# V^T of three quads packed into four transposes instead of six, at the end of their own quad

## The chip, the cores and the metric

The kernel runs on one core of one Trainium2 chip. The metric is the device time of one execution in microseconds (us). The kernel before takes 3127.38 us, the median of three runs (3127.18 to 3128.78). A core has five engines that matter here: TensorE (PE, with its weight loads as PEld), VectorE (DVE), ScalarE (ACT), GpSimd (POOL) and SyncE (SP), which issues most of the DMAs. Each engine works through its own queue in order, and semaphores make one wait for another.

## The reference

Two kinds of layers are applied in turn, A, B, A, B, each with a LayerNorm ahead and a residual sum behind. B has 32 heads of 20 with a dilated local window of 8 keys. A is an attention with 32 heads of 192 over segments of 32 tokens with 8 memory rows ahead of them; the memory rows' output is the memory of the next segment, so that the segments must be worked one after the other:

```python
for s in range(n_seg):                       # 64 segments of 32 tokens
    h = concat([mem, x[:, 32*s:32*(s+1)]])   # 8 + 32 = 40 rows
    q, k, v = (einsum('btd,dhe->bhte', h, W) for W in (Wq, Wk, Wv))
    p = softmax(where(mask, einsum('bhqe,bhke->bhqk', q, k) * 192**-0.5, -1e9))
    o = einsum('bhte,hed->btd', einsum('bhqk,bhke->bhqe', p, v), Wo)
    mem, out = o[:, :8], o[:, 8:]

x = x + A(layernorm(x)); x = x + B(layernorm(x))
x = x + A(layernorm(x)); x = x + B(layernorm(x))
```

The model width is 640, in five chunks of 128 (NC).

## The kernel before

The two A layers share their weights, and so do the two B layers. So the kernel works on two **lanes** at once: in step t, lane 0 does segment t of the first pair of layers and lane 1 does segment t-2 of the second pair. Each lane has 40 rows (LT) in layer A, so the two make 80 columns (NT). Steps 2 to 63 have both lanes; the first two and the last two have one (`one_lane`). Layer B of a step's output is worked one step later, spread over that step's quads.

Inside a step the 32 heads of layer A go in eight **quads** of four heads. Quad i runs, in the order in which `step` (L822) writes it down, and every engine keeps to the order in which its instructions are written there:

- `a_k`: 30 matmuls of 80 columns into bank 0 of PSUM. ACT copies the result to KF and Kz (three instructions, L309 to L311).
- `a_vt` (L344) of the quad **before**: six transposes of 128 columns (L351) turn V^T (`vT`, 6 pieces of 128 by 80) into V (`Vt`) by way of bank 2. One DVE copy (L353) takes 80 rows of 768 to `Vt`.
- `a_q`: 30 matmuls into bank 1. DVE copies them to QT (L316).
- `a_pv` of the quad before: eight matmuls with `Vt` as the stationary operand, over 80 rows. ACT makes the reciprocals R of the sums (L388, L390).
- `a_v`: 30 matmuls into bank 2. One DVE copy writes `vT` (L342).
- from quad 5 on, `a_o`: 30 matmuls of the output projection, five quads late.
- `a_norm` of the quad before (DVE, three instructions), which reads R.
- `a_s`: eight matmuls of the scores into bank 1. ACT takes the exponent E (L366).
- `a_mask`: DVE multiplies E with the mask (L372).

The rows of `Vt` and of E are keys. Both pairs of heads of a quad use rows 0 to 79 there, each in its own half of the columns.

The work of layer B stands between these: in quad 1 its Q and K projections (50 matmuls) and, on POOL, two multiplications that spread Q over heads (QX, L566); in quad 2 its V projection and, ahead of `a_pv`, its score group 0, whose matmuls (L581) write bank 0 (groups 0 and 2) or bank 3 (1 and 3); in quad 5 its second PV (L607). The normalisation of that (`b_norm(1)`: rB at L617, On at L622, on DVE) is written in quad 6 behind `a_k` and **ahead of** `a_vt`. The transposes of On (`b_ot`, L629) follow in quad 6 behind `a_q`. At the end of quad 6 stand `b_wo` (L640) and its two sums on DVE (xin, YT). At the end of quad 1, ACT's queue issues the load of the next x (L652) and in every second step the store of y (L655).

In quad 7 POOL makes the sums for the LayerNorm of the next step (L438 to L449), which read xin. TensorE adds them up (L467) ahead of `a_pv(7)`. Weights that don't fit are streamed by SP through a ring of four buffers (L249), as the matmuls that use them end.

Bank numbers come from tags; a tile of a bank is given out again when all reads of the one before have ended:

```python
ps = self.big(f"ps_{kind}", {"k": 0, "q": 1, "v": 2}[kind])   # proj, L290
ps = self.big("ps_bs", 3 * (g % 2))                           # b_s, L573
```

Of the kernel before, what the change touches and what calls it, by code (L numbers as in the profile page):

```python
# [10 lines left out]
BF16 = mybir.dt.bfloat16  # L11
F32 = mybir.dt.float32
ACT = mybir.ActivationFunctionType
ALU = mybir.AluOpType
# [3 lines left out]
P = 128  # L18
D = 640
NC = 5  # L20
DH = 192
NQUAD = 8
QE = 768
NM = 8
SEG = 32
# [12 lines left out]
BW = 8  # L38
# [7 lines left out]

MM = 5
VH = 512

def half_order():  # L50

# [27 lines left out]
class Kernel:  # L79
# [91 lines left out]

    def build_mask_a(self):
        nc, cp = self.nc, self.cp
        mA = cp.tile([P, NT], BF16, name="maskA")
        nc.gpsimd.memset(mA[:], 1.0)
        for l in range(2):
            c0 = LT * l
            nc.gpsimd.affine_select(out=mA[:, c0:c0 + NM], in_=mA[:, c0:c0 + NM], compare_op=ALU.is_ge, fill=0.0,
                                    base=c0 + LT - 1, pattern=[[0, NM]], channel_multiplier=-1)
            nc.gpsimd.affine_select(out=mA[:, c0 + NM:c0 + LT], in_=mA[:, c0 + NM:c0 + LT], compare_op=ALU.is_ge, fill=0.0,  # L180
                                    base=c0 + NM, pattern=[[1, SEG]], channel_multiplier=-1)
            nc.gpsimd.affine_select(out=mA[:, c0:c0 + LT], in_=mA[:, c0:c0 + LT], compare_op=ALU.is_ge, fill=0.0,
                                    base=-c0, pattern=[[0, LT]], channel_multiplier=1)
        self.maskA = mA

    def build_masks_b(self):
        nc, cp = self.nc, self.cp

        def band(name, cur):
            m = cp.tile([P, NX], BF16, name=name)  # L190
            nc.gpsimd.memset(m[:], 0.0)
            for half in range(2):
                off = 0 if half == cur else SEG
                for l in range(2):
                    r0 = 64 * half + SEG * l
                    blk = m[r0:r0 + SEG, SEG * l:SEG * (l + 1)]
                    for w in range(BW):
                        nc.gpsimd.affine_select(out=blk, in_=blk, compare_op=ALU.not_equal, fill=1.0,
                                                base=off - BDIL * w, pattern=[[1, SEG]], channel_multiplier=-1)
            return m  # L200

        self.maskB = [band("mB0", 0), band("mB1", 1)]
        f0 = cp.tile([P, NX], BF16, name="mB_f0")
        nc.gpsimd.tensor_copy(out=f0[:], in_=self.maskB[0][:])
        nc.gpsimd.memset(f0[64:64 + SEG, :], 0.0)
        f1 = cp.tile([P, NX], BF16, name="mB_f1")
        half1 = 1 - LAG % 2
        nc.gpsimd.tensor_copy(out=f1[:], in_=self.maskB[LAG % 2][:])
        nc.gpsimd.memset(f1[64 * half1 + SEG:64 * half1 + 2 * SEG, :], 0.0)
        self.maskB_first = {0: f0, LAG: f1}  # L210

        self.hmask = []
        for c, (h0, h1) in enumerate(B_HEADS):
# [121 lines left out]
    def a_v(self, i, t):  # L335

        self.v_rows = self.one_lane() and not 2 <= i <= 3
        if self.v_rows:
            return self.a_v_rows(i, t)
        nc = self.nc  # L340
        ps = self.proj("v", i, t)
        nc.vector.tensor_copy(out=self.cols(self.vT[:, 0:6 * NT].rearrange("p (a n) -> p a n", a=6)), in_=self.cols(ps[:, 0:6 * NT].rearrange("p (a n) -> p a n", a=6)))  # L342

    def a_vt(self):  # L344

        if self.v_rows:
            return
        nc = self.nc
        ps = self.ps_big.tile([P, 6, P], BF16, name="ps_vt", tag="bank2")
        for n in range(6):  # L350
            nc.tensor.transpose(out=ps[:, n, :], in_=self.vT[:, NT * n:NT * n + P], identity=self.ident[:])  # L351
        vt = self.Vt
        nc.vector.tensor_copy(out=vt[0:NT, :].rearrange("p (a b c) -> p a b c", a=2, b=2)[:, :, :, 0:DH],  # L353
                              in_=ps[0:NT].rearrange("p (a b) c -> p a (b c)", a=2).rearrange("p a (b c) -> p a b c", b=2))

    def a_s(self):
        nc = self.nc
        ps = self.big("ps_s", 1)
        sv = ps[:, 0:4 * NT].rearrange("p (h n) -> p h n", h=4)
        kf, kz, qt = self.KF, self.Kz, self.qt  # L360
        for h in range(4):
            pr, j = h // 2, h % 2
            nc.tensor.matmul(self.cols(sv[:, h]), lhsT=kf[:, NT * h:NT * h + P], rhs=self.cols(qt[:, 3 * pr + 2 * j]), start=True, stop=False)  # L363
            nc.tensor.matmul(self.cols(sv[:, h]), lhsT=kz[:, NT * h:NT * h + P], rhs=self.cols(qt[:, 3 * pr + 1]), start=False, stop=True)  # L364
        e = self.ap1.tile([P, 4, NT], BF16, name="E")
        nc.scalar.activation(out=self.cols(e[0:NT]), in_=self.cols(sv[0:NT]), func=ACT.Exp, scale=float(DH) ** -0.5)  # L366
        self.em = e

    def a_mask(self):
        nc, e = self.nc, self.em  # L370
        n = self.c1 - self.c0
        nc.vector.tensor_tensor(out=self.cols(e[0:NT]), in0=self.cols(e[0:NT]),  # L372
                                in1=self.cols(self.maskA[0:NT, :]).unsqueeze(1).to_broadcast([NT, 4, n]), op=ALU.mult)

    def a_pv(self):

# [4 lines left out]
        ov = ops[:, :, 0:4 * NT].rearrange("p a (k n) -> p a k n", k=4)  # L381
        for pr in range(2):
            for k, c0 in enumerate((0, 128, 192, 320)):
                nc.tensor.matmul(self.cols(ov[:, pr, k]), lhsT=vt[0:NT, VH * pr + c0:VH * pr + c0 + P], rhs=self.cols(em[0:NT, 2 * pr + k // 2]), start=True, stop=True)  # L384
# [437 lines left out]
    def step(self, t):  # L822
# [6 lines left out]
        for i in range(NQUAD - 1):  # L829
            self.a_k(i, t)  # L830
            if b is not None and i == 6:
                self.b_norm(1)
            if i >= 1:
                self.a_vt()
            if b is not None and i == 1:
                self.b_ln_apply(b)
            if b is not None and i == 3:
# [16 lines left out]
                self.b_pv(1)  # L854
            if i >= 1:
                self.a_norm(i - 1)
            self.a_s()
            if b is not None and i == 0:
                self.b_ln(b)
            self.a_mask()  # L860
# [18 lines left out]
        self.a_v(7, t)  # L879
        self.a_o(7 - OLAG)  # L880
        self.a_norm(6)
        self.a_s()
        self.a_vt()
        self.a_mask()
        self.a_o(8 - OLAG)
        self.a_o(9 - OLAG, slice(0, NC), False)
# [102 lines left out]
```

## Time and profile before

| | |
|---|---|
| runs (median, lowest, highest) | 3127.38, 3127.18, 3128.78 us |
| profiled execution | span of 3128.7 us, the only time that the page gives for it |
| busy: PE, PEld, DVE, ACT, POOL | 98%, 97%, 76%, 59%, 18% |
| granted TensorE clock, mean | 0.993 |
| DMA | 785.02 MB, 251 GB/s on the mean |
| transposes of `a_vt` | 3024 |
| copies vT, Vt (DVE) | 504 each |

A row of a group has line, engine, operation, names (out<-in), shapes and count; then, behind the bar, busy us and the mean ns of one, and then the idle time ahead of them with what ended it. A row of a timeline has start and length in us, engine, line, operation and names, a count where like instructions follow each other, and in brackets the idle time of the engine ahead of it and what ended it. The length of a matmul row includes the way through the array, so matmuls that follow each other overlap; the start of the next row tells when TensorE was free again. ACTq and SPq rows are DMA issues.

### The profile page before, as it was taken

What the parts mean: (1) busy time and instruction counts of PE and PEld (TensorE: products, weight loads), DVE (VectorE), ACT (ScalarE), POOL (GpSimd) and SP (SyncE); (2) the same over time, 40 slices, a digit from 0 to 9 for tenths busy, and PEclk for the clock granted to TensorE, in tenths of its full rate; (3) what the DMA queues carried; (4) which work ended last, traced back from release to release, by engine and by line L of the source; (5) the groups of instructions that cost most, each with busy time, mean ns of one, the idle gap of its engine ahead of it and who ended that gap; (6) DMA issues with size and microseconds to landing.
All of it is one profiled execution on the core that took longest, in us unless ns stands there. A gap on an engine that the chain in (4) does not pass through costs nothing.

```text
span 3128.7 us, 187179 instructions
## 1 busy us (share of the span) xinstructions
PE 3079.1 (98%) x83454; PEld 3030.8 (97%) x83454; DVE 2369.5 (76%) x6009; ACT 1845.1 (59%) x5612; POOL 553.2 (18%) x1028
## 2 busy tenths in 40 slices
PE   6999999999999999999999999999999999999998
PEld 4899999999999999999999999999999999999997
DVE  3677777777777777777777777777777777877776
ACT  2556656656656656656656656656656656655654
POOL 2111111111111111111111111111111111111121
PEclk7999999999999999999999999999999999999999
DMA  9877777777777777777777777777777777777776
GB/s 392 287 246 248 246 246 239 250 243 246 249 244 249 246 246 250 247 247 247 247 246 248 248 245 249 250 246 245 250 246 248 249 244 249 250 243 250 248 251 219
DMA packets 452970, 785.02 MB, mean 251 GB/s; under 512 B 58560, under 2 KB 444352, under 8 KB 452160
## 3 DMA queue, kind: packets, MB, share of 16 engines
q1 hardware_dynamic: 438480, 767.84, 76.4%
q8 instruction: 652, 10.68, 1.4%
q10 hardware_dynamic: 13680, 5.21, 0.7%
q14 instruction: 158, 1.29, 0.1%
HBM read 770.22 MB, written 2.62 MB: 247 GB/s over the span
## 4 chain that ended last, share of the span: by engine, by line
PE 96%; DMA 3%; issue 1%; ACT 0%; DVE 0%; SPq 0%; ACTq 0%
PE ps_k L297 18%; PE ps_acc L415 18%; PE ps_q L297 17%; PE ps_v L297 17%; PE ps_vt L351 5%; PE ps_o L384 5%; PE ps_s L363 2%; PE ps_s L364 2%; PE ps_bs L581 2%; PE ps_bk L529 2%; PE ps_by L640 2%; PE ps_bq L529 1%; PE ps_bv L529 1%; PE ps_vr L331 1%; PE ps_bo L607 1%
## 5 line engine op out<-in xcount | busy, mean ns | idle before, releaser
L388 ACT ACTIVATE R<-ps_o 64x160 f32<-64x160 f32 (+1 forms) x2112 | 620.1, 294 | 338.4 <-PE ps_o L384 122.8
L297 PEld LDWEIGHTS <-w_ring 128*128 128x128 bf16 x16470 | 676.6, 100 | 18.7 <-issue 5.3
L297 PE MATMUL ps_q<-hT,w_q 128*128 128x80 bf16 (+1 forms) x12870 | 541.1, 201 | 4.8 <-DMA w_q<-in_A_Wq_dram 4.2
L566 POOL TENSOR_TENSOR QX<-QB,hmask 128x448 bf16<-128x448 bf16 (+2 forms) x325 | 304.5, 945 | 1338.2 <-ACT QB L544 1025.1
L297 PEld LDWEIGHTS <-w_q 128*128 128x128 bf16 x12870 | 493.8, 100 | 6.0 <-DMA w_q<-in_A_Wq_dram 5.3
L309 ACT CAST KF<-ps_k 128x320 bf16<-128x320 f32 (+1 forms) x528 | 218.5, 414 | 414.7 <-PE ps_k L297 399.1
L415 PE MATMUL ps_acc<-OT,w_o 128*128 128x80 bf16 (+1 forms) x9900 | 458.9, 201 | 3.7 <-DMA w_o<-in_A_Wo_dram 2.3
L342 DVE CAST vT<-ps_v 128x480 bf16<-128x480 f32 (+1 forms) x504 | 329.3, 653 | 166.2 <-PE ps_v L297 148.1
L316 DVE CAST QT<-ps_q 128x480 bf16<-128x480 f32 (+1 forms) x528 | 337.5, 639 | 119.7 <-PE ps_q L297 116.5
L297 PE MATMUL ps_v<-hT,w_v 128*128 128x80 bf16 (+1 forms) x9480 | 423.7, 201 | 4.1 <-issue 2.4
L415 PEld LDWEIGHTS <-w_o 128*128 128x128 bf16 x9900 | 393.2, 100 | 5.4 <-DMA w_o<-in_A_Wo_dram 2.9
L297 PE MATMUL ps_k<-hT,w_k 128*128 128x80 bf16 (+1 forms) x7920 | 373.5, 201 | 2.9 <-DMA w_k<-in_A_Wk_dram 2.7
L297 PEld LDWEIGHTS <-w_v 128*128 128x128 bf16 x9480 | 371.6, 100 | 4.9 <-issue 2.9
L297 PE MATMUL ps_k<-hT,w_ring 128*128 128x80 bf16 (+1 forms) x7860 | 370.5, 201 | 5.4 <-issue 3.4
L366 ACT ACTIVATE E<-ps_s 80x320 bf16<-80x320 f32 (+1 forms) x528 | 220.7, 418 | 241.4 <-PE ps_s L364 240.1
L398 DVE TENSOR_TENSOR OT<-ps_o,R 128x320 bf16<-128x320 f32 (+1 forms) x528 | 254.1, 481 | 135.4 <-ACT R L390 115.7
L297 PEld LDWEIGHTS <-w_k 128*128 128x128 bf16 x7920 | 321.5, 100 | 3.7 <-DMA w_k<-in_A_Wk_dram 3.1
L353 DVE COPY Vt<-ps_vt 80x768 bf16<-80x768 bf16 x504 | 279.0, 554 | 56.4 <-PE ps_vt L351 44.5
L415 PE MATMUL ps_acc<-OT,w_ring 128*128 128x80 bf16 (+1 forms) x5940 | 307.9, 201 | 1.5 <-issue 1.1
L297 PE MATMUL ps_v<-hT,w_ring 128*128 128x80 bf16 (+1 forms) x5640 | 264.8, 202 | 0.8 <-DMA w_ring<-in_A_Wv_dram 0.7
L372 DVE TENSOR_TENSOR E<-E,maskA 80x320 bf16<-80x320 bf16 (+1 forms) x528 | 207.0, 392 | 64.7 <-ACT E L366 54.0
L390 ACT ACTIVATE R<-R 128x320 f32<-128x320 f32 (+1 forms) x528 | 244.1, 462 | 16.7
(159 smaller groups left out, 4932.2 us busy)
## 6 DMA issues: line engine op xcount, KB each, us to landing
w_ring<-in_A_Wk_dram SPq DMA_DIRECT2D x1036, 240.0 KB, 3.7
w_ring<-in_A_Wo_dram SPq DMA_DIRECT2D x780, 240.0 KB, 3.8
w_ring<-in_A_Wv_dram SPq DMA_DIRECT2D x776, 240.0 KB, 4.0
w_ring<-in_A_Wq_dram SPq DMA_DIRECT2D x390, 240.0 KB, 4.0
w_q<-in_A_Wq_dram SPq DMA_DIRECT2D x5, 960.0 KB, 11.0
w_v<-in_A_Wv_dram SPq DMA_DIRECT2D x6, 480.0 KB, 11.3
w_ring<-in_A_Wk_dram SPq DMA_DIRECT2D x6, 480.0 KB, 10.2
w_ring<-in_A_Wo_dram SPq DMA_DIRECT2D x6, 480.0 KB, 11.3
```

Source lines behind the costliest of these rows:

```text
L297: nc.tensor.matmul(ps[:, NT * n + self.c0:NT * n + self.c1], lhsT=w[n // 3][:, c, P * (n % 3):P * (n % 3 + 1)], rhs=hT[:, NT * c + self.c0 ...
L309: nc.scalar.copy(out=kf, in_=pv[:, :, 0:3:2, :])
L316: self.nc.vector.tensor_copy(out=self.cols(qt[:]), in_=self.cols(ps[:, 0:6 * NT].rearrange("p (a n) -> p a n", a=6)))
L342: nc.vector.tensor_copy(out=self.cols(self.vT[:, 0:6 * NT].rearrange("p (a n) -> p a n", a=6)), in_=self.cols(ps[:, 0:6 * NT].rearrange("p ...
L353: nc.vector.tensor_copy(out=vt[0:NT, :].rearrange("p (a b c) -> p a b c", a=2, b=2)[:, :, :, 0:DH], in_=ps[0:NT].rearrange("p (a b) c -> p ...
L366: nc.scalar.activation(out=self.cols(e[0:NT]), in_=self.cols(sv[0:NT]), func=ACT.Exp, scale=float(DH) ** -0.5)
L372: nc.vector.tensor_tensor(out=self.cols(e[0:NT]), in0=self.cols(e[0:NT]), in1=self.cols(self.maskA[0:NT, :]).unsqueeze(1).to_broadcast([NT ...
L388: nc.scalar.activation(out=self.cols(r[r0:r0 + 64, :, j]), in_=self.cols(src), func=ACT.Ln)
L390: nc.scalar.activation(out=rf, in_=rf, func=ACT.Exp, scale=-1.0)
L398: nc.vector.tensor_tensor(out=oc[:, :, 0:3:2], in0=ov[:, :, 0:4:3], in1=r, op=ALU.mult)
L415: nc.tensor.matmul(self.cols(acc[:, k]), lhsT=w[m // 3][:, m % 3, P * c:P * (c + 1)], rhs=self.cols(ot[:, m]), start=(i == 0 and m == 0 an ...
L566: self.nc.gpsimd.tensor_tensor(out=qx[:, 0:nh, self.on], in0=self.qb[:, c, self.on].unsqueeze(1).to_broadcast([P, nh, n]), in1=self.hmask[ ...
```

## The change

In the quads 1, 5 and 6 (`PACKED`), in steps with both lanes, V^T is packed before it is transposed. The 80 keys of the two pairs make 6 pieces of 80 columns. The new layout puts 64 keys of both pairs next to each other in each of three blocks of 128 columns, and the 16 keys left of each of the six pieces in a fourth block of 96. So four transposes do, in place of six.

For this the second pair of heads moves to rows 48 to 127 of `Vt` and E (`PK` = 48): the stationary slices of KF and Kz in `a_s` begin 48 columns earlier for it, exponent, mask and PV cover 128 rows, and the mask of layer A is built for both positions. The vT copy on DVE becomes two (64 and 16 keys). Behind the transposes, DVE copies the fourth block to a new tile `Vx`, and the three main blocks to `Vt` in two instructions, one for each pair. ACT takes the 16 keys of the first pair from `Vx` to `Vt` in three copies, and POOL those of the second pair in three (32 rows; 16 of them fall on rows that the mask of E makes zero).

In these quads `a_vt(i)` stands at the end of quad i itself, behind `a_mask(i)` (in quad 6 behind `b_wo`), in place of behind `a_k(i + 1)`. It stands ahead of the x load and the y store in quad 1.

Two masks of layer B that only the first steps used are dropped; the second half of the first mask is now built in two pieces, by eight selects on POOL each, at the end of quad 6 in steps 1 and 3.

```diff
+PK = P - NT
+PACKED = (1, 5, 6)
...
+        self.Vx = pers("Vx", [P, P], 1, zero=False)[0]
...
     def a_v(self, i, t):
...
         ps = self.proj("v", i, t)
+        if self.packed(i):
+            at = lambda o, pr, n: bass.AP(ps.tensor, ps[:, o:].offset, [list(ps[:].ap[0]), [NT, 3], [pr, 2], [1, n]])
+            part = lambda c0, n: self.vT[:, c0:c0 + 6 * n].rearrange("p (b a n) -> p b a n", b=3, a=2)
+            nc.vector.tensor_copy(out=part(0, 64), in_=at(0, 3 * NT + 16, 64))
+            nc.vector.tensor_copy(out=part(3 * P, 16), in_=at(64, 3 * NT - 64, 16))
+            return
...
+    def packed(self, i):
+        return i in PACKED and not self.one_lane()
...
-    def a_vt(self):
+    def a_vt(self, i):
...
+        vt = self.Vt
+        if self.packed(i):
+            ps = self.ps_big.tile([P, 4, P], BF16, name="ps_vt", tag="bank2")
+            for n in (3, 0, 1, 2):
+                nc.tensor.transpose(out=ps[:, n, :], in_=self.vT[:, P * n:P * (n + 1)], identity=self.ident[:])
+            src = ps[:, 0:3].rearrange("p a b -> p (a b)").rearrange("p (b c) -> p b c", b=2)
+            dst = vt[:].rearrange("p (a b c) -> p a b c", a=2, b=2)[:, :, :, 0:DH]
+            nc.vector.tensor_copy(out=self.Vx[0:96], in_=ps[0:96, 3, :])
+            nc.vector.tensor_copy(out=dst[0:64, 0], in_=src[0:64])
+            halves = lambda v: v.rearrange("p (b c) -> p b c", b=2)
+            for a in range(2):
+                copy = nc.gpsimd.tensor_copy if a else nc.scalar.copy
+                r0, n = ((64, 16), (32, 32))[a]
+                row = vt[r0:r0 + n, VH * a:VH * (a + 1)]
+                copy(out=row[:, 0:128], in_=self.Vx[0:n])
+                copy(out=halves(row[:, 128:384])[:, :, 0:64], in_=halves(self.Vx[32:32 + n]))
+                copy(out=row[:, 320:448], in_=self.Vx[64:64 + n])
+            nc.vector.tensor_copy(out=dst[64:P, 1], in_=src[64:P])
+            return
...
-    def a_s(self):
+    def a_s(self, i):
+        self.rows = P if self.packed(i) else NT
...
+            k0 = NT * h - PK * (pr if self.packed(i) else 0)
...
-        mask = self.maskB_first.get(b, self.maskB[b % 2])
+        mask = self.maskB[b % 2]
...
-            if i >= 1:
-                self.a_vt()
+            if i >= 1 and not self.packed(i - 1):
+                self.a_vt(i - 1)
...
             if b is not None and i == 6:
                 self.b_wo(b)
+            if self.packed(i):
+                self.a_vt(i)
+            if b in (0, LAG) and i == 6:
+                self.band_block(self.maskB[0], 1, 0, int(b == LAG))
...
-        self.a_vt()
+        if not self.packed(6):
+            self.a_vt(6)
...
-        self.a_vt()
+        self.a_vt(7)
```

More of the change, by code (lines that the diff above doesn't have):

```diff
@@ L173, in build_mask_a, with band_block @@
         nc, cp = self.nc, self.cp
-        mA = cp.tile([P, NT], BF16, name="maskA")
+        mA = cp.tile([P, 2, NT], BF16, name="maskA")
         nc.gpsimd.memset(mA[:], 1.0)
-        for l in range(2):
+        for a, l in ((a, l) for a in range(2) for l in range(2)):
             c0 = LT * l
[L178 to L183, printed above, removed]
-        self.maskA = mA
+            r0 = c0 + PK * a
+            nc.gpsimd.affine_select(out=mA[:, a, c0:c0 + NM], in_=mA[:, a, c0:c0 + NM], compare_op=ALU.is_ge, fill=0.0,
+                                    base=r0 + LT - 1, pattern=[[0, NM]], channel_multiplier=-1)
+            nc.gpsimd.affine_select(out=mA[:, a, c0 + NM:c0 + LT], in_=mA[:, a, c0 + NM:c0 + LT], compare_op=ALU.is_ge, fill=0.0,
+                                    base=r0 + NM, pattern=[[1, SEG]], channel_multiplier=-1)
+            nc.gpsimd.affine_select(out=mA[:, a, c0:c0 + LT], in_=mA[:, a, c0:c0 + LT], compare_op=ALU.is_ge, fill=0.0,
+                                    base=-r0, pattern=[[0, LT]], channel_multiplier=1)
+        self.maskA = mA
+    def band_block(self, m, half, cur, l):
+        r0 = 64 * half + SEG * l
+        blk = m[r0:r0 + SEG, SEG * l:SEG * (l + 1)]
+        for w in range(BW):
+            self.nc.gpsimd.affine_select(out=blk, in_=blk, compare_op=ALU.not_equal, fill=1.0,
+                                         base=(0 if half == cur else SEG) - BDIL * w, pattern=[[1, SEG]], channel_multiplier=-1)
     def build_masks_b(self):
@@ L191, in band @@
             nc.gpsimd.memset(m[:], 0.0)
[L192 to L199, printed above, removed]
+            for l in range(2):
+                self.band_block(m, cur, cur, l)
             return m
         self.maskB = [band("mB0", 0), band("mB1", 1)]
[L203 to L210, printed above, removed]
+        for l in range(2):
+            self.band_block(self.maskB[1], 0, 1, l)
         self.hmask = []
@@ L371, in a_mask @@
         n = self.c1 - self.c0
+        if self.rows == P:
+            nc.vector.tensor_tensor(out=e[:].rearrange("p (a j) n -> p a j n", a=2), in0=e[:].rearrange("p (a j) n -> p a j n", a=2),
+                                    in1=self.maskA[:].unsqueeze(2).to_broadcast([P, 2, 2, NT]), op=ALU.mult)
+            return
         nc.vector.tensor_tensor(out=self.cols(e[0:NT]), in0=self.cols(e[0:NT]),
-                                in1=self.cols(self.maskA[0:NT, :]).unsqueeze(1).to_broadcast([NT, 4, n]), op=ALU.mult)
+                                in1=self.cols(self.maskA[0:NT, 0]).unsqueeze(1).to_broadcast([NT, 4, n]), op=ALU.mult)
     def a_pv(self):
@@ L383, in a_pv @@
             for k, c0 in enumerate((0, 128, 192, 320)):
-                nc.tensor.matmul(self.cols(ov[:, pr, k]), lhsT=vt[0:NT, VH * pr + c0:VH * pr + c0 + P], rhs=self.cols(em[0:NT, 2 * pr + k // 2]), start=True, stop=True)
+                nc.tensor.matmul(self.cols(ov[:, pr, k]), lhsT=vt[0:self.rows, VH * pr + c0:VH * pr + c0 + P], rhs=self.cols(em[0:self.rows, 2 * pr + k // 2]), start=True, stop=True)
         r = self.ap1.tile([P, 2, 2, NT], F32, name="R")
@@ L856, in step @@
                 self.a_norm(i - 1)
-            self.a_s()
+            self.a_s(i)
             if b is not None and i == 0:
@@ L881, in step @@
         self.a_norm(6)
-        self.a_s()
-        self.a_vt()
+        self.a_s(7)
+        self.a_vt(7)
         self.a_mask()
```

7 lines of the change are left out of this document (3 added, 4 removed).

## The prediction

> **What bounds the kernel now.** I read the page's busy shares first, then the chain of work that ended last, then one step by windows, and last the timelines of the engines around the three moved blocks.
>
> ```profile
> span 3128.7 us, 187179 instructions
> PE 3079.1 (98%) x83454; PEld 3030.8 (97%) x83454; DVE 2369.5 (76%) x6009; ACT 1845.1 (59%) x5612; POOL 553.2 (18%) x1028
> ...
> PE 96%; DMA 3%; issue 1%; ACT 0%; DVE 0%; SPq 0%; ACTq 0%
> ```
>
> ```profile
> 2003.93:2050.64 46.71, 46.71 (x1276) 46.43 (x1273) 36.40 (x91) 28.36 (x85) 8.23 (x14) 1.00 0.77 246
> ```
>
> The second fence is one step with both lanes (columns: stretch, its length, then busy time and count of PE, PEld, DVE, ACT, POOL, granted clock, DMA share, GB/s). TensorE is busy for all 46.71 us of it, at the full clock. So TensorE is the bound, at no slack, and every wait that the change puts in front of a matmul is paid in full. There are 62 such steps (t = 2 to 63); the others run with one lane, where nothing is packed. DVE is busy for 36.40 of the 46.71 us and ACT for 28.36, but in queue order: their slack is not everywhere.
>
> **What the change takes away, and the prices.** These are rows of the groups by line and shape.
>
> ```profile
> L351 PE MATMUL ps_vt<-ident,vT 128*128 128x128 bf16 x3024 | 253.4, 220 | 0.3 <-issue 0.2
> L384 PE MATMUL ps_o<-E,Vt 80*128 80x80 bf16 x3968 | 225.3, 201 | 0.0
> L363 PE MATMUL ps_s<-QT,KF 128*128 128x80 bf16 x1984 | 206.9, 202 | 0.5 <-ACT R L388 0.3 <-issue 0.2
> L353 DVE COPY Vt<-ps_vt 80x768 bf16<-80x768 bf16 x504 | 279.0, 554 | 56.4 <-PE ps_vt L351 44.5
> L559 DVE COPY VB<-ps_bvt 128x320 bf16<-128x320 bf16 x132 | 36.4, 322 | 0.5 <-PE ps_bvt L555 0.5
> L342 DVE CAST vT<-ps_v 128x480 bf16<-128x480 f32 x496 | 326.0, 657 | 159.4 <-PE ps_v L297 141.3
> L316 DVE CAST QT<-ps_q 128x240 bf16<-128x240 f32 x32 | 13.0, 406 | 25.1 <-PE ps_q L297 24.9
> L484 ACT ACTIVATE ln_r<-ln_v 128x64 f32<-128x64 f32 x131 | 33.6, 257 | 4.2
> L390 ACT ACTIVATE R<-R 128x320 f32<-128x320 f32 x496 | 233.3, 470 | 15.7
> L632 ACT CAST OTB<-ps_bt 64x64 bf16<-64x64 f32 x65 | 13.5, 207 | 2.1
> L448 POOL CAST ln_h<-ln_s 128x128 bf16<-128x128 f32 x65 | 18.8, 290 | 4.2
> L198 POOL TENSOR_SCALAR_AFFINE_SELECT mB<-mB 32x32 bf16<-32x32 bf16 x64 | 13.3, 212 | 3.4
> ```
>
> The gain: two transposes of six in three quads of 62 steps, 372 in all. Six follow each other in 0.335 us (2014.22 to 2014.55 in the next fence), 0.056 us each, so 0.335 us a step and 20.8 us in all. Score, PV and exponent instructions stay as many and as wide; that they use 128 partitions in place of 80 I cost at nothing: the PV matmuls on 80 take 201 ns, the score matmuls on 128 take 202.
>
> DVE copies from PSUM in bf16 cost 0.155 us plus 0.52 ns an element (from the 768 and 320 element rows): 0.22 us for Vx (128), 0.355 us for each half of the main copy (384). The vT cast in two parts costs 0.56 and 0.255 us (a line through 480 and 240 elements). An ACT copy of 128 elements out of SBUF is not in the trace: bounds 0.207 (64 elements from PSUM) and 0.470 (320 from SBUF); the line between the two SBUF rows, 0.257 and 0.470, gives 0.31, which I take because they have the same source, and three of them follow each other end to end, 0.93 us. [...] A POOL copy of 128 elements lies between 0.21 (the 32-element select) and 0.43 (two inputs of 128, the last row of place C); I take the cast of 128, 0.29, so 0.87 us for three.
>
> **Place A, quad 1 into quad 2.** The timelines of one step, engine by engine:
>
> ```profile
> 2014.22 0.50 PE L351 MATMUL ps_vt<-ident,vT 128*128 128x128 bf16 x6
> 2014.55 1.24 PE L297 MATMUL ps_q<-hT,w_q 128*128 128x80 bf16 x30
> ...
> 2016.36 0.41 PE L581 MATMUL ps_bs<-QX,KB 128*128 128x448 bf16 x2
> ```
>
> ```profile
> 2013.85 0.99 DVE L372 TENSOR_TENSOR E<-E,maskA 80x320 bf16<-80x320 bf16 x1 [0.51 <-ACT E L366]
> 2014.87 0.55 DVE L353 COPY Vt<-ps_vt 80x768 bf16<-80x768 bf16 x1
> ```
>
> ```profile
> 2013.40 0.34 ACTq L652 DMA_DIRECT2D xin<-in_A_x_dram  x1
> 2014.42 0.42 ACT L309 CAST KF<-ps_k 128x320 bf16<-128x320 f32 x1 [0.61 <-PE ps_k L297]
> ...
> 2015.04 0.29 ACT L311 CAST Kz<-ps_k 64x160 bf16<-64x160 f32 x1
> ```
>
> ```profile
> 2012.83 1.82 POOL L566 TENSOR_TENSOR QX<-QB,hmask 128x448 bf16<-128x448 bf16 x2 [15.15 <-ACT QB L544]
> ```
>
> The mask of quad 1 takes 0.99 us, against 0.32 us in the other quads (rows below), because it stands beside the two QX instructions on POOL, which end at 2014.65; it ends at 2014.84. The packed copies come behind it on DVE: Vx from 2014.88 to 2015.10. ACT's three copies wait for Vx, and KF and Kz of quad 2 are queued behind them: the copies run from 2015.13 to 2016.06, then KF and Kz take their 0.91 us (2014.42 to 2015.33 now) and end at 2016.97. The first score group of layer B (L581, group 0) writes bank 0, which KF and Kz of quad 2 read, so it waits for them. TensorE would come to it at 2016.36 less 0.11, that is 2016.25. Today KF and Kz are done 1.0 us before it; after the change they are 0.72 us late, with the handover (0.06, an estimate: the mask row at 2045.74 ends 0.14 us before the matmuls that use it, with no wait) **0.78 us a step**. With ACT copies of 0.207 it is 0.47, of 0.470 it is 1.26.
>
> Also queued behind the waiting copies are the loads of x (0.34 us of issue) and every second step the store of y:
>
> ```profile
> L655 ACTq DMA_DIRECT2D out_dram<-YT x32: 338/446/1878, 277.5 to 3125.6; - x32
> ```
>
> Issue of both, 0.34 + 0.45 us, runs beside the three copies; only a store near its longest, 1.88 us, would hold KF further. I allow 3 us in all (0 to 12). The loaded x is wanted some 25 us later. POOL's copies end at about 2016.0, ahead of the PV matmuls that need them. SP's prefetches follow the matmuls and are not moved past anything.
>
> **Place B, quad 5 into quad 6.**
>
> ```profile
> 2033.84 0.32 DVE L372 TENSOR_TENSOR E<-E,maskA 80x320 bf16<-80x320 bf16 x1 [0.24 <-ACT E L366]
> 2034.20 0.21 DVE L617 RECIPROCAL rB<-ps_bo 128x8 f32<-128x8 f32 x1
> 2034.44 0.66 DVE L622 TENSOR_TENSOR On<-ps_bo,rB 64x160 bf16<-64x160 f32 x2
> 2035.12 0.56 DVE L353 COPY Vt<-ps_vt 80x768 bf16<-80x768 bf16 x1
> ```
>
> ```profile
> 2035.66 0.33 PE L629 MATMUL ps_bt<-ident,On 128*128 128x128 bf16 x3
> ```
>
> Today layer B's second normalisation (rB, On) runs ahead of the Vt copy of quad 5. At the end of its own quad, the copy moves ahead of it: Vx, and both halves of the main copy, start to start 0.15 + 0.385 + 0.385 = 0.92 us. On ends at 2036.02 in place of 2035.10. The transposes of On would start at 2035.66 less 0.11, so 2035.55: **0.53 us late**, handover included (0.35 to 0.65 as the three copies overlap more or less). ACT's and POOL's copies are hidden here: KF of quad 6 is needed three microseconds later.
>
> **Place C, quad 6 into quad 7**, told in the times of before, as place B's wait moves all of it alike.
>
> ```profile
> 2040.27 0.31 DVE L649 TENSOR_TENSOR YT<-ps_by,x 128x160 bf16<-128x160 f32 x1
> ```
>
> ```profile
> 2042.31 1.23 ACT L388 ACTIVATE R<-ps_o 64x160 f32<-64x160 f32 x4 [0.84 <-ACT Kz L311]
> ```
>
> ```profile
> 2041.77 0.46 PE L384 MATMUL ps_o<-E,Vt 80*128 80x80 bf16 x8
> ...
> 2046.09 0.28 PE L467 MATMUL ps_st<-ln_h,ones 128*128 128x128 bf16 x2
> 2046.20 0.45 PE L384 MATMUL ps_o<-E,Vt 80*128 80x80 bf16 x8
> ```
>
> ```profile
> 2045.15 0.55 DVE L353 COPY Vt<-ps_vt 80x768 bf16<-80x768 bf16 x1
> 2045.74 0.32 DVE L372 TENSOR_TENSOR E<-E,maskA 80x320 bf16<-80x320 bf16 x1
> ```
>
> ```profile
> 2040.49 0.72 POOL L438 TENSOR_TENSOR sq<-xin 128x320 bf16<-128x320 bf16 x1 [18.10 <-issue]
> ...
> 2043.97 0.43 POOL L449 TENSOR_TENSOR ln_h<-ln_s,ln_h 128x128 bf16<-128x128 f32 x1
> ```
>
> Vx follows YT, 2040.51 to 2040.73. ACT's copies end at 2041.70, POOL's at 2041.64; PV of quad 6, due at 2041.77 less 0.11, waits 0.10 us. KF and Kz end at 2042.61, so R starts 0.32 us later than now, and all that follows R (normalisation, Vt, mask of quad 7) runs end to end up to PV of quad 7, which has 0.08 us to spare: it waits 0.25 us. **0.35 us** together; 0.1 with the short ACT copies, 1.1 with the long ones. POOL's LayerNorm sums are moved 1.15 us back, to end at 2045.55, 0.54 us before the matmuls that need them: hidden.
>
> In steps 1 and 3 eight selects (2 us by L198) stand ahead of these sums: about 2 us once. In the prologue masks are built beside the first weight loads: nothing.
>
> **The sum.** 0.78 + 0.53 + 0.35 - 0.335 = 1.33 us a step, 82 us for 62, with 2 and 3 once, 87. The profiled execution spans 3128.7 us, 1.3 above the median of the runs, 3127.4; on the median it gives **3214 us**.
>
> **The rivals.** (1) *Only place B waits*, as bank 0 or ACT's queue gives way at A: then C goes too, since it hangs on the same ACT copies, and 0.53 - 0.335 over 62 steps gives 3140. The queue of B is plain; against it, KF stands behind the copies in the order of the program. (2) *POOL becomes the bound in C*: copies there move 32 partitions to others, which no row has. Above 0.45 us each, LayerNorm's sums end behind the matmuls that wait for them; at QX's 0.94 it is 1.5 us a step more, 3300 us. The nearest row, 0.29, speaks against it. [...] (3) *Faster*: ACT and DVE take KF and On ahead of the new copies. Then nothing waits, and 20.8 us are gained: 3107 us. It decides where less than 0.5 us goes ahead of On and less than 1.0 us ahead of KF. Against it: at place A Vt ran only behind the mask, at 2014.87, though its transposes were done at 2014.72, so DVE kept its order.
>
> **How the numbers follow.** Forecast 0.78, rival 1 0.09, rival 2 0.06, rival 3 0.05, and 0.02 that gains and waits cancel within 0.2% (6 us, what a measurement here can tell). The forecast's ends: short ACT copies give 0.47 + 0.35 + 0.1 - 0.335, 36 us; long ones 1.26 + 0.65 + 1.1 - 0.335, 166 us. The range takes in rival 1 below and leaves out the far upper end, where all three prices would be long at once: 3138 to 3260. Slower 0.93, same 0.02, faster 0.05.
>
> **What would show it.** In the waits of after: L581's successor with ACT Kz as releaser, about 48 us; the transposes of On with DVE On, 33 us; PV with ACT or POOL copies and the mask, 22 us. Transposes fall from 3024 to 2652. DVE grows by about 0.9 us a packed quad. If TensorE is idle at A for under 0.2 us, or On does not come behind the copies, the forecast is wrong.

## The result, and the profile after

The kernel after takes 3204.56 us, the median of five runs (3202.99 to 3211.42); the kernel before, beside it, 3127.38 us. The ratio is 1.0249, with a 95% interval of 1.0237 to 1.0262: 77 us slower, where 87 were forecast. The profiled execution took 3203.59 us, its span 3201.9 us.

The profile page's busy time and its chain of work that ended last, of the kernel after:

```profile
span 3201.9 us, 188236 instructions
...
PE 3088.2 (96%) x83082; PEld 3023.4 (94%) x83082; DVE 2432.2 (76%) x6567; ACT 2020.1 (63%) x6170; POOL 709.2 (22%) x1588
...
PE 78%; DVE 12%; ACT 5%; DMA 2%; issue 2%; ACTq 1%; POOL 0%; SPq 0%; DVEq 0%; POOLq 0%
```

TensorE has 372 instructions less (83082 against 83454), as forecast. But the chain, which lay on TensorE for 96% before, now runs through DVE for 12% and through ACT for 5% of the span. DVE's busy share stands still at 76%: no engine has become full; TensorE waits. One step with both lanes, by windows:

```profile
2050.44:2098.41 47.97, 46.89 (x1271) 46.30 (x1268) 37.40 (x100) 31.18 (x94) 10.74 (x23) 1.00 0.75 240
```

It is 47.97 us long, 1.26 more than the 46.71 before (forecast 1.33), at the same full clock. The waits view of the kernel after (who waits for whom: us in total, times, longest) names three places:

```profile
PE ps_bs L615 <- ACT Kz L311: 36.7, 60, 1.5
...
PE ps_bt L663 <- DVE On L656: 18.4, 59, 0.3
...
PE ps_o L418 <- DVE E L406: 10.2, 59, 0.2
```

L615, L663 and L418 are L581, L629 and L384 of the kernel before. Each wait comes about 60 times, once in a step with both lanes. The view counts from the end of the matmul ahead, but a row of 80 columns lasts 0.20 us (L393, mean) while the next one starts 0.036 us behind its start; what a wait costs is read better from the starts. So from here on a wait is the time by which a matmul starts later than the usual spacing behind the one ahead (the median in the kernel after: 0.036 us for 80 columns, 0.056 for 128), summed over the 62 steps. That gives 46.8 us at L615 (0.755 a step), 28.4 at L663 (0.457) and 20.3 at L418 (0.327). Together 95.5 us, less the 20.8 of the transposes saved, is 74.7; the 62 steps are together 75.0 us longer (2980.1 against 2905.1).

The same step on the engines' timelines. **Place A**, quad 1 into quad 2 (TensorE, DVE, POOL, ACT):

```profile
2062.03 0.89 PE L563 MATMUL ps_bv<-h2T,wb_sb 128*128 128x64 bf16 x25
2063.52 0.42 PE L615 MATMUL ps_bs<-QX,KB 128*128 128x448 bf16 x2 [0.60 <-ACT Kz L311]
```

```profile
2060.37 0.98 DVE L403 TENSOR_TENSOR E<-E,maskA 128x320 bf16<-128x320 bf16 x1 [0.51 <-ACT E L396]
```

```profile
2059.34 1.82 POOL L600 TENSOR_TENSOR QX<-QB,hmask 128x448 bf16<-128x448 bf16 x2 [14.06 <-ACT QB L578]
```

```profile
2061.64 0.29 ACT L373 COPY Vt<-Vx 16x128 bf16<-16x128 bf16 x1 [1.30 <-DVE Vx L366]
...
2062.55 0.43 ACT L309 CAST KF<-ps_k 128x320 bf16<-128x320 f32 x1
...
2063.17 0.29 ACT L311 CAST Kz<-ps_k 64x160 bf16<-64x160 f32 x1
```

This is the chain that was forecast, link by link: the mask lasts 0.98 us beside QX, and Vx is queued behind it; ACT idles 1.30 us for Vx, its three copies run end to end, and KF and Kz behind them end at 2063.46. TensorE's 25 matmuls of layer B's V projection are out at 2062.76 (0.029 us each), so L615 starts 0.76 us late.

**Place B**, quad 5 into quad 6, and **place C**, quad 6 into quad 7:

```profile
2081.38 0.22 DVE L366 COPY Vx<-ps_vt 96x128 bf16<-96x128 bf16 x1
...
2081.88 0.36 DVE L376 COPY Vt<-ps_vt 64x384 bf16<-64x384 bf16 x1
2082.25 0.21 DVE L651 RECIPROCAL rB<-ps_bo 128x8 f32<-128x8 f32 x1
2082.49 0.66 DVE L656 TENSOR_TENSOR On<-ps_bo,rB 64x160 bf16<-64x160 f32 x2
```

```profile
2083.20 0.33 PE L663 MATMUL ps_bt<-ident,On 128*128 128x128 bf16 x3 [0.31 <-DVE On L656]
...
2089.19 0.46 PE L418 MATMUL ps_o<-E,Vt 128*128 128x80 bf16 x8
...
2093.51 0.28 PE L501 MATMUL ps_st<-ln_h,ones 128*128 128x128 bf16 x2
2093.96 0.45 PE L418 MATMUL ps_o<-E,Vt 80*128 80x80 bf16 x8 [0.17 <-DVE E L406]
```

```profile
2088.90 0.29 ACT L375 COPY Vt<-Vx 16x128 bf16<-16x128 bf16 x1
2089.22 0.43 ACT L309 CAST KF<-ps_k 128x320 bf16<-128x320 f32 x1
...
2089.84 0.29 ACT L311 CAST Kz<-ps_k 64x160 bf16<-64x160 f32 x1
2090.15 1.23 ACT L422 ACTIVATE R<-ps_o 64x160 f32<-64x160 f32 x4
```

```profile
2093.59 0.32 DVE L406 TENSOR_TENSOR E<-E,maskA 80x320 bf16<-80x320 bf16 x1
```

In B the three copies (0.87 us, start to start) stand between the mask and rB, and On's transposes start 0.47 us late. In C, PV of quad 6 (2089.19) doesn't wait; R stands in ACT's queue behind the copies, KF and Kz. The normalisation, the Vt copy and the mask of quad 7 come behind R, and the mask ends at 2093.91. So the wait comes out at PV of quad 7: 2093.96, where 2093.62 was due.

The groups by line and shape give the prices of the new instructions:

```profile
L367 DVE COPY Vt<-ps_vt 64x384 bf16<-64x384 bf16 x186 | 63.2, 340 | 0.0
...
L374 ACT COPY Vt<-Vx 16x128 bf16<-16x128 bf16 x186 | 55.0, 295 | 3.8
...
L374 POOL COPY Vt<-Vx 32x128 bf16<-32x128 bf16 x186 | 53.1, 286 | 10.7
...
L366 DVE COPY Vx<-ps_vt 96x128 bf16<-96x128 bf16 x186 | 40.5, 218 | 3.9
```

### The profile page after: what moved, and what is told of

Read it like the earlier page. It is cut to its first block, busy times and chain, and to the rows that moved or that the text cites. A ratio compares the mean times of both kernels' runs of the same rounds, so it can differ in the third digit from the quotient of the medians.

```text
span 3201.9 us, 188236 instructions
## 1 busy us (share of the span) xinstructions
PE 3088.2 (96%) x83082; PEld 3023.4 (94%) x83082; DVE 2432.2 (76%) x6567; ACT 2020.1 (63%) x6170; POOL 709.2 (22%) x1588
## 3 DMA queue, kind: packets, MB, share of 16 engines
q1 hardware_dynamic: 438480, 767.84, 74.7%
## 4 chain that ended last, share of the span: by engine, by line
PE 78%; DVE 12%; ACT 5%; DMA 2%; issue 2%; ACTq 1%; POOL 0%; SPq 0%; DVEq 0%; POOLq 0%
PE ps_v L297 17%; PE ps_acc L449 15%; PE ps_k L297 13%; PE ps_q L297 13%; PE ps_o L418 5%; PE ps_vt L380 3%; DVE E L403 2%; PE ps_bs L615 2%; PE ps_s L394 2%; PE ps_s L393 2%; ACT E L396 2%; PE ps_by L674 1%; DVE OT L434 1%; DVE On L656 1%; DVE Vt L381 1%
## 5 line engine op out<-in xcount | busy, mean ns | idle before, releaser
L297 PEld LDWEIGHTS <-w_ring 128*128 128x128 bf16 x16470 | 675.4, 100 | 14.8 <-issue 2.7
L396 ACT ACTIVATE E<-ps_s 80x320 bf16<-80x320 f32 (+2 forms) x528 | 222.2, 421 | 213.4 <-PE ps_s L394 213.4
L373 POOL COPY Vt<-Vx 32x128 bf16<-32x128 bf16 x186 | 52.6, 283 | 1142.1 <-DVE Vx L366 799.3
L348 DVE CAST vT<-ps_v 128x480 bf16<-128x480 f32 (+1 forms) x318 | 206.8, 650 | 89.2 <-PE ps_v L297 89.2
L449 PEld LDWEIGHTS <-w_ring 128*128 128x128 bf16 x5940 | 248.4, 100 | 2.3 <-DMA w_ring<-in_A_Wo_dram 0.5
```

Source lines behind the costliest of these rows:

```text
L297: nc.tensor.matmul(ps[:, NT * n + self.c0:NT * n + self.c1], lhsT=w[n // 3][:, c, P * (n % 3):P * (n % 3 + 1)], rhs=hT[:, NT * c + self.c0 ...
L396: nc.scalar.activation(out=self.cols(e[0:self.rows]), in_=self.cols(sv[0:self.rows]), func=ACT.Exp, scale=float(DH) ** -0.5)
L449: nc.tensor.matmul(self.cols(acc[:, k]), lhsT=w[m // 3][:, m % 3, P * c:P * (c + 1)], rhs=self.cols(ot[:, m]), start=(i == 0 and m == 0 an ...
```

## The experiments

The theory: the loss is three separate waits, each made by the order of instructions on one queue, and the packing's own work would fit beside the rest. The main rival: six more copies, a wider mask and a second vT cast in each packed quad load DVE, ACT and POOL, and cost about the same wherever they stand.

The waits measured in every run, in us over the 62 steps with both lanes. Only waits of over 0.06 us each count, and groups under 0.8 us in total are left out. So are scattered stalls of up to some 4 us a run at one kind of matmul, which the kernel before has too. The sums are good to about 1 us. Times are medians. The kernel before was run again beside each run and took 3124 to 3128 us; where two runs are compared below, it is by their distance from the kernel before beside each.

| run | time | before, beside it | ratio, 95% interval | A: score group 0 | B: On's transposes | C: PV of quad 7 | other places |
|---|---|---|---|---|---|---|---|
| after | 3204.56 | 3127.38 | 1.0249 (1.0237 to 1.0262) | 46.8 | 28.4 | 20.3 | LayerNorm sums 2.0 |
| x_q1 | 3172.16 | 3128.45 | 1.0134 (1.0119 to 1.0149) | 45.3 | 0 | 0 | |
| x_q5 | 3148.15 | 3128.45 | 1.0055 (1.0039 to 1.0072) | 0 | 28.8 | 0 | |
| x_q6 | 3145.78 | 3128.45 | 1.0048 (1.0033 to 1.0063) | 0 | 0 | 18.5 | LayerNorm sums 2.0 |
| e_place | 3130.33 | 3128.45 | 1.0004 (0.9994 to 1.0015) | 0 | 0 | 0 | |
| e_vx | 3152.64 | 3124.40 | 1.0091 (1.0076 to 1.0106) | 2.5 | 28.6 | 19.4 | LayerNorm sums 2.0 |
| e_kf | 3152.89 | 3124.40 | 1.0092 (1.0077 to 1.0107) | 0 | 28.5 | 20.1 | PV of quad 1 2.9, LayerNorm sums 2.0 |
| e_on | 3252.46 | 3124.40 | 1.0411 (1.0395 to 1.0426) | 46.9 | 0 | 20.3 | PV of quad 5 34.3, of quad 6 42.7, LayerNorm sums 2.0 |
| e_c | 3181.08 | 3124.40 | 1.0177 (1.0160 to 1.0194) | 48.5 | 28.6 | 0 | LayerNorm sums 1.4 |
| v2 | 3106.58 | 3126.56 | 0.9939 (0.9927 to 0.9952) | 2.2 | 0 | 0 | |
| v4 | 3169.52 | 3126.56 | 1.0142 (1.0127 to 1.0158) | 2.7 | 0 | 0 | transposes of quad 0 36.0, of quad 4 43.1 |
| v3 | 3350.76 | 3126.56 | 1.0719 (1.0705 to 1.0734) | 1.2 | 10.1 | 0 | transposes of four quads 165.3, score group 2 86.9, PV of quads 4 and 5 14.9 |
| v5 | 3157.00 | 3127.87 | 1.0098 (1.0082 to 1.0115) | 1.3 | 12.7 | 0 | PV of quad 4 43.6, of quad 5 3.2 |

### One quad at a time, and the place without the packing

x_q1, x_q5 and x_q6 change one line of the kernel after:

```diff
-PACKED = (1, 5, 6)
+PACKED = (1,)        # x_q1; (5,) in x_q5, (6,) in x_q6
```

> Only quad 1 packed (PACKED = (1,)). Theory (three separate waits, each set by the order of one queue): place A's wait stays whole, 0.75 us a step as in the trace after, less 0.112 us for two transposes, so 0.64 x 62 = 40 us, with 2 us for the selects 3127 + 42 = 3169 us; no wait at On's transposes nor at PV of quad 7. Rival (the extra copies simply load DVE, ACT and POOL, wherever they stand): a third of the whole difference of 77 us, 3153 us.

> Only quad 5 packed. Theory: place B's wait alone, 0.455 us a step as in the trace after, less 0.112, so 0.34 x 62 = 21 us, with 2 us for the selects 3150 us. Rival (general load): a third of 77 us, 3153 us; this run tells the two apart only together with those of quads 1 and 6.

> Only quad 6 packed. Theory: place C's wait alone, 0.33 us a step as in the trace after, less 0.112, so 0.22 x 62 = 13.5 us, with 2 us for the selects 3143 us. Rival (general load): a third of 77 us, 3153 us.

Measured: 43.7, 19.7 and 17.3 us over the kernel before, together 81, about the whole (77), and each time within some 3 us of the one expected. The equal share of the rival, 26 us or a ratio of 1.0083, lies outside all three intervals. Each run has its own wait only, as large as in the kernel after. In the waits views of x_q1, x_q5 and x_q6, one each:

```profile
PE ps_bs L615 <- ACT Kz L311: 35.3, 59, 1.6
```

```profile
PE ps_bt L663 <- DVE On L656: 18.4, 60, 0.4
```

```profile
PE ps_o L418 <- DVE E L406: 8.8, 54, 0.2
```

So the three waits don't depend on each other, and the terms of the sum may be added. That C comes without B's wait ahead of it, and as large to within 2 us, was assumed in the prediction.

e_place keeps the six transposes and the one copy of the kernel before, but moves those of the three quads to the end of their own quad:

```diff
+    def early(self, i):
+        return i in (1, 5, 6) and not self.one_lane()
     def packed(self, i):
-        return i in PACKED and not self.one_lane()
+        return False
...
-            if self.packed(i):
+            if self.early(i):
                 self.a_vt(i)
```

> Nothing packed: six transposes and one copy as in the kernel before, but those of quads 1, 5 and 6 at the end of their own quad. Theory (the packed copies make the waits, the place alone costs little): at A nothing on ACT's queue, no wait; at B one copy of 0.47 us, start to start, ahead of rB and On, 0.39 us of which they had to spare, so about 0.1 us a step; at C nothing. With the selects 3127 + 6 + 2 = 3135 us (3127 to 3140). Rival (the place is what costs): most of the 77 us, 3180 us or more.

It is as fast as the kernel before: none of the three places has a wait. The place costs nothing by itself; what costs is the packed copies at that place. The 0.1 us a step that was allowed at B, and the 2 us for the selects, don't show. At B the one copy (0.47 us from start to start in the kernel before, L353 at 2009.16 and the next instruction at 2009.63) found room ahead of rB and On.

### Place A: which link holds it

e_vx moves the transposes and Vx of quad 1 ahead of the mask. e_kf leaves Vx where it is and writes ACT's copies behind KF and Kz of quad 2. (`a_vt` is cut into parts for both: t the transposes, x Vx, d0 and d1 the main copies, a and p the copies of ACT and POOL.)

```diff
 e_vx:
+            if i == 1 and self.packed(i):
+                self.a_vt(i, "t x")
             self.a_mask()
...
             if self.packed(i):
-                self.a_vt(i)
+                self.a_vt(i, "d0 a p d1" if i == 1 else "t x d0 a p d1")
 e_kf:
             self.a_k(i, t)
+            if i == 2 and self.packed(1):
+                self.a_vt(1, "a")
...
             if self.packed(i):
-                self.a_vt(i)
+                self.a_vt(i, "t x d0 p d1" if i == 1 else "t x d0 a p d1")
```

> The changed kernel, with quad 1's four transposes and its Vx written ahead of the mask of quad 1; its other copies stay behind. Theory (place A is the chain of queues: slow mask, then Vx, then ACT's copies, then KF): Vx is ready about 1.2 us earlier, ACT's copies end before KF's data are there, place A's 0.75 us a step go: 3205 - 46 = 3158 us. Rival (ACT has 1.8 us of copies there, and that length decides wherever Vx stands): the wait moves to PV of quad 1 or stays, 3190 us or more.

> The changed kernel, with ACT's three copies of quad 1 written behind KF and Kz of quad 2 instead of ahead of them. Theory: bank 0 comes free in time, but the copies now end 2.07 us behind the end of the K projection, and PV of quad 1, which needs them, is due 1.49 us behind it: a wait of about 0.6 us takes the place of 0.75, 3205 - 7 = 3198 us. Rival (KF's place in ACT's queue is all of it): the whole 0.75 go, 3158 us.

e_vx: A's wait falls from 46.8 to 2.5 us, the time by 49 us. The slow mask ahead of Vx is a necessary link; the length of ACT's copies alone is not enough to make the wait. e_kf came out as its rival had it, and I was wrong: the wait goes too, and PV of quad 1 waits only 2.9 us in all. My expectation had left out 25 matmuls of layer B's V projection, 0.73 us, that stand between the Q projection and PV in quad 2. ACT and TensorE in e_kf:

```profile
2077.69 0.43 ACT L309 CAST KF<-ps_k 128x320 bf16<-128x320 f32 x1 [0.82 <-PE ps_k L297]
...
2079.14 0.29 ACT L382 COPY Vt<-Vx 16x128 bf16<-16x128 bf16 x1
```

```profile
2078.57 0.90 PE L571 MATMUL ps_bv<-h2T,wb_sb 128*128 128x64 bf16 x25
2079.30 0.41 PE L623 MATMUL ps_bs<-QX,KB 128*128 128x448 bf16 x2
```

The copies end at 2079.43; the scores start without a wait at 2079.30, and PV follows 0.25 us behind them. So KF's place behind copies that wait is all of A, and two different reorderings remove it: of the transposes and Vx on TensorE and DVE in e_vx, of ACT's queue alone in e_kf.

### Place B: On ahead of the copies

```diff
             if self.packed(i):
+                if i == 5:
+                    self.b_norm(1)
                 self.a_vt(i)
...
-            if b is not None and i == 6:
+            if b is not None and i == 6 and not self.packed(5):
                 self.b_norm(1)
```

> The changed kernel, with rB and On written ahead of the packed copies of quad 5. Theory: On's transposes wait no longer, but Vx starts 0.9 us later, ACT's copies behind it end about 0.65 us after PV of quad 5 is due: the wait changes its place and grows from 0.455 to about 0.65, 3205 + 12 = 3217 us. Rival (the copies of quad 5 are hidden there, only On is late): 0.455 us a step go, 3205 - 28 = 3177 us.

On's wait is gone, and the kernel is 51 us slower, where 12 were expected. A wait at PV of quad 5 comes in its place, as expected: 34.3 us over the steps, 0.55 a step, where 0.65 was expected. What I hadn't foreseen is the next one, 42.7 us at PV of quad 6. ACT and DVE in a step of e_on show it:

```profile
2163.50 0.29 ACT L382 COPY Vt<-Vx 16x128 bf16<-16x128 bf16 x1
2163.82 0.43 ACT L309 CAST KF<-ps_k 128x320 bf16<-128x320 f32 x1
...
2165.49 1.23 ACT L430 ACTIVATE R<-ps_o 64x160 f32<-64x160 f32 x4
```

```profile
2167.26 0.49 DVE L440 TENSOR_TENSOR OT<-ps_o,R 128x320 bf16<-128x320 f32 x1 [1.17 <-ACT R L432]
...
2169.17 0.21 DVE L372 COPY Vx<-ps_vt 96x128 bf16<-96x128 bf16 x1
```

ACT's late copies push KF, OTB and R of quad 5 behind them, end to end. R holds the normalisation, that holds the mask and Vx of quad 6, and Vx the copies that PV of quad 6 needs. The order of the kernel after was the cheaper of the two.

### Place C: the copies ahead of the mask

```diff
+            if i == 6 and self.packed(i):
+                self.a_vt(i, "t x a p")
             self.a_mask()
...
             if self.packed(i):
-                self.a_vt(i)
+                self.a_vt(i, "d0 d1" if i == 6 else "t x d0 a p d1")
```

> The changed kernel, with quad 6's transposes, Vx and ACT's and POOL's copies written ahead of its mask and of layer B's output projection; the two main copies stay where they are. Theory (place C comes from ACT's copies ahead of KF of quad 7, which pushes R and all behind it): the copies end before KF's data are there, and 0.33 us a step go: 3205 - 20 = 3184 us. Rival (the two extra DVE instructions of the packed quad, or the shifted main copies, make PV of quad 7 late): 3200 us or more.

The time falls by 20 us, and C's wait is gone, though both main copies still stand behind YT. The edit moves Vx and POOL's copies too; what singles out ACT's queue is R, which now waits for PV of quad 6 and not for Kz:

```profile
2122.40 1.23 ACT L430 ACTIVATE R<-ps_o 64x160 f32<-64x160 f32 x4 [0.41 <-PE ps_o L426]
```

So it was ACT's late copies ahead of KF, not the main copies on DVE.

### All three reordered

v2 takes e_vx and e_c together, and at B it splits the copies around rB and On:

```diff
             if b is not None and i == 6:
                 self.b_norm(1)
+            if i == 6 and self.packed(5):
+                self.a_vt(5, "d1")
...
+            if self.packed(i):
+                self.a_vt(i, "t x a p" + (" d0" if i == 5 else ""))
             self.a_mask()
...
-            if self.packed(i):
-                self.a_vt(i)
...
+            if self.packed(i) and i != 5:
+                self.a_vt(i, "d0 d1")
```

The eight selects of steps 1 and 3 move behind POOL's LayerNorm sums.

> Quads 1, 5 and 6 packed, with the order on the queues changed: in all three Vx and ACT's and POOL's copies stand ahead of the quad's mask, in quad 5 the first main copy too, and its second one behind rB and On; in quad 6 the transposes stand ahead of layer B's output projection; the selects of steps 1 and 3 stand behind POOL's LayerNorm sums. Theory (all the loss is waits of order, none the work itself): no place waits, and the 20.8 us of the transposes are gained, 3127 - 21 = 3106 us (3103 to 3115). Rival (three copies on ACT and POOL can't be had beside the rest): some wait of 0.1 to 0.5 us a step is left, 3115 to 3140 us.

3106.58 us, 0.6% faster than the kernel before and 3% faster than the kernel after: the whole gain of the transposes. A step with both lanes, by windows, and place B on DVE and on TensorE:

```profile
1985.95:2032.33 46.38, 46.38 (x1271) 46.10 (x1268) 37.21 (x100) 31.07 (x94) 10.99 (x23) 1.00 0.77 246
```

```profile
2015.57 0.22 DVE L372 COPY Vx<-ps_vt 96x128 bf16<-96x128 bf16 x1
2015.71 0.34 DVE L374 COPY Vt<-ps_vt 64x384 bf16<-64x384 bf16 x1
2016.08 0.33 DVE L411 TENSOR_TENSOR E<-E,maskA 128x320 bf16<-128x320 bf16 x1
...
2016.56 0.66 DVE L664 TENSOR_TENSOR On<-ps_bo,rB 64x160 bf16<-64x160 f32 x2
```

```profile
2017.46 0.33 PE L671 MATMUL ps_bt<-ident,On 128*128 128x128 bf16 x3
```

TensorE is busy for all of 46.38 us, 0.33 less than before, and DVE, ACT and POOL do the same number of instructions as in the kernel after (100, 94 and 23 in the step). Only their order differs. DVE idled 0.22 us ahead of quad 5's mask in the kernel after; Vx now stands in that gap.

### More quads

v4 packs quads 0 and 4 too, and v3 all of 0 to 6, in the order of v2. v5 is v2 with quad 4 packed, but with its transposes behind the K projection of quad 5, where they stood in the kernel before, and its copies ahead of KF of that quad.

```diff
-PACKED = (1, 5, 6)
+PACKED = (0, 1, 4, 5, 6)          # v4; (0, 1, 2, 3, 4, 5, 6) in v3; (1, 4, 5, 6) in v5
 v5, in a_k:
+LATE = (4,)
...
         ps = self.proj("k", i, t)
+        if i - 1 in LATE and self.packed(i - 1):
+            self.a_vt(i - 1, "t x a p d0 d1")
```

> As the run before, with quads 0 and 4 packed too. Theory: two more transposes in two more quads, 0.224 us a step or 13.9 us, 3092 us. Rival: in quad 0 ACT's copies stand ahead of the two instructions of layer B's LayerNorm, and in quad 4 they push KF and R of quad 5; a wait there takes the gain, 3106 us or more.

> As the run before, with quads 2 and 3 packed too, seven in all. Theory: 0.112 us a step and quad, 48.6 us in all, 3079 us. Rival: in quads 2 and 3 ACT also has layer B's four exponents of 0.6 us, so that KF of the next quad comes late for the score groups that write bank 0; 0.2 to 0.5 us a step are lost there, 3090 to 3125 us.

> The version with quads 1, 5 and 6 reordered, and quad 4 packed too, but with its transposes where they stood in the kernel before, behind the K projection of quad 5; all its copies stand ahead of KF of quad 5. Theory (in quad 4 too little TensorE work stands between the V projection and the end of the quad, so that the transposes waited 0.69 us a step for the two vT casts; a projection further on the casts are covered): no wait at the transposes, ACT's copies end about when PV of quad 4 is due, KF of quad 5 is 1.3 us late and wanted 3 us later, so 0.112 us a step is gained, 3107 - 7 = 3100 us. Rival (the copies, started that late, make PV of quad 4 or R behind KF late): 3107 to 3140 us.

All three lost. In v4 the places that I had named do nothing; a new one waits, the transposes themselves. TensorE and DVE in quad 4:

```profile
2005.32 0.20 PE L402 MATMUL ps_s<-QT,Kz 128*128 128x80 bf16 x1
2006.05 0.40 PE L365 MATMUL ps_vt<-ident,vT 128*128 128x128 bf16 x4 [0.53 <-DVE vT L346]
```

```profile
2005.27 0.56 DVE L345 CAST vT<-ps_v 128x384 bf16<-128x384 f32 x1 [0.37 <-PE ps_v L297]
2005.75 0.25 DVE L346 CAST vT<-ps_v 128x96 bf16<-128x96 f32 x1
```

Between the V projection and the end of quad 4 stand only the eight score matmuls, 0.29 us (in quad 0 two short matmuls of a LayerNorm more, 0.11 us); the two casts of vT take 0.73. In quad 1 two projections of layer B stand between them (50 matmuls, 0.029 us each), in quads 5 and 6 the output projection of an earlier quad (30 matmuls, 0.036 us each). That cover made the early transposes free in the three packed quads, and it is missing in the others; the time of v4 agrees (79.1 us of waits less 13.9 gained, against 63 us measured over v2). v3 loses the same at four quads, and 86.9 us more at layer B's score group 2 in quad 3, which waits for Kz behind the copies, as its rival had it; but the rival's price was 0.2 to 0.5 us a step, and this wait alone is 1.4. In v5 the transposes don't wait, but Vx stands behind the casts, the normalisation and the mask, on a DVE that is busy end to end (2089.96 to 2094.51); ACT's copies come 0.7 us late for PV of quad 4, and R behind them pushes On, which the transposes in quad 6 need. The 3157 us lie above the range of the rival too. Neither of the two places tried in quad 4 is free.

## Why the prediction was right, point by point

- **The gain**, 20.8 us: right. v2 shows it alone, 0.33 us a step. So scores, exponent and PV over 128 rows cost the step nothing, as assumed: in the kernel after a PV matmul takes 201 ns over 80 rows and over 128 (L418), the exponent 422 and 439 (L396).
- **Place A**, 0.78 us a step: 0.755. All links and their order were right, from the slow mask to KF. The excess is in one price: the three ACT copies, taken as 0.93 us, hold KF back by 0.91 (2061.64 to 2062.55). One copy lasts 0.295 us, but what KF paid for each is the time from start to start, 0.30 to 0.32 us. My 0.31 was worked out as a duration, so that it came out near the spacing is luck. At place C the three copies take 0.96 us (2088.26 to 2089.22), more than the price.
- **Place B**, 0.53: 0.457, inside its bounds of 0.35 to 0.65. The three copies take 0.87 us start to start, not 0.92, and the wait in the step shown is 0.47. The mean over the steps is lower still, as stalls ahead of it hide in it (last section).
- **Place C**, 0.35: 0.327, but not as two parts. The 0.10 at PV of quad 6 doesn't exist: it starts as ACT's last copy ends (2089.19) and a little before POOL's last one does (2089.26), whose rows only its last four matmuls use. The whole lateness comes out at PV of quad 7. e_c confirms the cause, ACT's copies ahead of KF and R.
- **The selects**, 2 us once: 2.0 at the LayerNorm sums, in step 3 alone, where they stand behind POOL's copies of quad 6. In x_q1 and x_q5, where quad 6 isn't packed, the same selects cost nothing. **The y store**, 3 us: seen in a few steps only. In the longest of them, on ACT's queue in the kernel after:

```profile
2974.70 1.41 ACTq L689 DMA_DIRECT2D out_dram<-YT  x1
...
2976.14 0.43 ACT L309 CAST KF<-ps_k 128x320 bf16<-128x320 f32 x1 [0.93 <-PE ps_bv L563]
```

  KF waits for the end of the issue (2976.11), and score group 0 waits 0.9 us longer there than in the other steps. The row names a matmul as the releaser, which had long been done.
- **Rival 1** (only B waits): wrong, since A and C have their waits. **Rival 2** (POOL becomes the bound): wrong, a POOL copy takes 0.29 us, as assumed from the cast of 128. From start to start it is 0.34 to 0.36, but the LayerNorm sums still end 0.26 us ahead of the matmuls that need them. **Rival 3** (faster, 3107 us): wrong for this order, and its time is that of v2, 3106.6 us. The engines kept their written order, as argued; v2 gets the gain by writing another one.

- **The signs**: transposes fell to 2652, and A and B named the releasers that were written down; PV of quad 7 named the mask alone. One sign was wrong: DVE was to grow by 0.9 us a packed quad, and it grew by 0.34 (2432.2 against 2369.5 us busy, over 186 quads). The prediction's own prices give 0.53; its sum didn't use this figure.

In sum, the terms that were mis-sized are small: 0.025, 0.07 and 0.02 us a step, 7 us in all, the 3 us for the store of which about 1 shows, and some microseconds of spread between runs.

## What to carry to other kernels

Here TensorE was the bound, busy for all 46.71 us of a step, and the order on the other engines' queues decided what the saved TensorE work was worth: 3204.56 us in one order, 3106.58 in another, with the same number of instructions in the step. So for each new instruction, look for what is queued behind it and when TensorE comes for that, and not at the engine's busy share. The three short copies of place A, on an engine with 40% of its time free, cost 46.8 us, more than twice the 20.8 that the saved transposes gave, and 2.2 in v2, where they were written ahead of a slow instruction (the mask of 0.98 us) instead of behind it. An operation moved to an earlier place also needs its inputs there (in v4 the transposes waited 36.0 and 43.1 us for theirs): the packing was free in the three quads, of seven tried, that have more TensorE work behind the V projection than the 0.73 us of the casts.

## What the runs showed of the hardware beyond the expected

Where instructions of DVE and POOL overlapped, now the one and now the other lasted longer. The mask of quad 1 (two SBUF inputs) lasts 0.98 us beside POOL's QX, against 0.33 in the other packed quads. In e_c, where POOL's first copy and quad 6's mask overlap, it is POOL's that is longer: its copy lasts 0.44 us, against 0.28 in the kernel after (L373, mean), and the mask keeps its 0.33:

```profile
2120.12 0.33 DVE L411 TENSOR_TENSOR E<-E,maskA 128x320 bf16<-128x320 bf16 x1
```

```profile
2120.15 0.44 POOL L380 COPY Vt<-Vx 32x128 bf16<-32x128 bf16 x1 [4.79 <-DVE Vx L372]
```

The copy of Vx, whose source is PSUM, took no more time there: that of quad 1 in v2 (1995.60) ran beside QX (1994.86 to 1996.69) in 0.22 us, as in the other quads.

A wait also hid other stalls. In one step of the kernel after, TensorE stood idle for 0.26 us in quad 6, ahead of On's transposes, for nothing that the profile shows (`issue`):

```profile
2034.32 0.45 PE L297 MATMUL ps_q<-hT,w_ring 128*128 128x80 bf16 x8 [0.26 <-issue]
...
2035.20 0.33 PE L663 MATMUL ps_bt<-ident,On 128*128 128x128 bf16 x3
```

The transposes then waited no longer for On, and the step took 48.00 us, as long as its neighbours (47.96 and 47.97). Here a stall ahead of a wait cost nothing; that it would count with the wait gone is argued, not run.
